# A planned two-branch attention kernel: V products of 512 columns, a limit on filler work, moves of Q and K on two queues, v swapped in one transfer

## The chip, the core and the metric

The kernel runs on one core of a Trainium2 chip. The metric is the device time of one launch in microseconds (us). The kernel before took 2022.6 us (median of three runs, 2015.66 to 2030.31). The engines are named as the profile names them: PE (TensorE, matmuls), PEld (its weight loads), DVE (VectorE), ACT (ScalarE), POOL (GpSimd), SP (SyncE, which here only issues transfers).

## The reference, cut to what matters

Two attention branches over the same x of 2048 rows and 512 columns are mixed row by row by a gate. Both have 32 heads of width 16. In branch a all heads share one k and one v; in branch b each head has its own.

```python
g = sigmoid((x * gate_w).sum(-1, keepdims=True))
# a: q = x @ wq (32 heads), k = x @ wk, v = x @ wv (one head of width 16)
# b: q, k, v = x @ wqkv (32 heads each)
scores = einsum("bhqd,b[h]kd->bhqk", q, k) * 16 ** -0.5
o = einsum("bhqk,b[h]kd->bhqd", softmax(scores), v)
out = g * (o_a @ wo_a) + (1 - g) * (o_b @ wo_b)
```

## The kernel before, in words

The 64 heads of the two branches are eight groups of eight heads, `groups` = a0, b0, a1, b1, ... Each group is worked in four phases (a half of the query rows, times two pairs of heads), so there are 32 phases. A phase has 32 quads: a quad is one tile of 128 keys (16 of them, `c`), in one of two arrangements of rows (`w`). A quad has two scores. One score is eight matmuls of 64x32 weights over 512 columns (L564) into one of two PSUM tiles `sc`, and one exponential of 128x1024 elements on ACT (L571) that writes a `prob` tile. Then the quad's V product (`values`, L612) multiplies v (with columns of ones, which give the denominators) by the quad's two `prob` tiles and adds into a PSUM tile `pair` for the whole phase. The product is in f32; the profile shows each of its matmuls as two instructions with a weight load each. Before the change a quad's V product is made in two pieces of 256 columns (`value_job`, L628).

Some scores don't go to ACT: the planner hands a whole quad to DVE, which makes the exponential from seven vector instructions (L751 to L763). Its matmuls go to the second `pair` tile, the spare bank; its V product is made in four pieces of 128 columns.

All other matmul work also goes through the spare bank, one piece of work at a time. It is kept as *units*: a projection of q, k or v (24 jobs of eight matmuls, L188; `project`, L371), the turning of v by transposes (16 jobs, L420; `turned`, L414), a product with wo (6 jobs, L188; `o_unit`, L445). A projection ends with two DVE instructions (L394, L397) that split the result into two f16 halves `hi` and `lo`, a single pair of buffers. `put` (L380) then lays them into the row order that the scores need by 32 transfers of 32 KB, issued at L352, all by POOL. `hi` and `lo` are free for the next projection when these are done (`free["hilo"]`). For v, `turned` writes `vB[0]` and copies it with its 64-row halves exchanged into `vB[1]` (`swapped`, L191, by SP): two calls, one for each of the two columns blocks that hold v, two transfers each.

After a phase, DVE copies the sum out (L665), SP moves numerators and denominators by ten transfers into tiles `oT` and `dT` (`normalised`, L505), DVE divides. Four `o_unit`s for each half of a group multiply by wo; DVE applies the gate (L471) into one of two `sum` tiles, and POOL adds them to the output in memory by a transfer that accumulates (L481).

Weights come in by SP (L216, L219), POOL splits them into halves (L204 to L206), and SP exchanges their 64-row halves (`halve`, L224, L193). DVE takes their largest value for a range check (L197). A second `_general` kernel stands behind that check and isn't entered here.

The order in which every engine gets its instructions is written by a planner that runs while the kernel is built. It keeps a model of the clocks of PE, DVE, POOL and ACT (`_Plan`, L77) with fixed costs (L44 to L49 and the numbers in the calls), and at each step emits what would fit. `pe_step` (L843) emits a score as soon as the modelled ACT has emptied its PSUM tile. Until then it emits filler work that ends before `limit` (L858), the modelled start of the last exponential plus `SLACK`: V products of ACT's quads first (`mine`), then jobs of units or scores for DVE (`spare`), then V products of DVE's quads (`other`). `spare_job` (L804) prefers a score for DVE to a unit, except when a unit that can start is within `SPARE` of being late by the model (`hurry`, L795). `pick` (L686) chooses the quad for DVE, at times in the next phase. Each engine works its list in order, whatever the real times are.

Of the kernel before, what the change touches and what calls it, by code (L numbers as in the profile page):

```python
# [44 lines left out]
SCORES, HALF, PRODUCT = 215, 430, 215  # L45
SLACK = 400
TO_VEC, FROM_VEC, CHAINED = 255, 150, 130
ISSUE, LANDS = 520, 3200
PROBS, VECS = 6, 7  # L49
# [27 lines left out]
class _Plan:  # L77


    def __init__(self):  # L80
        self.pe = self.dve = self.pool = self.act = 0.0
        self.starts, self.ends, self.ops, self.last = [], [], [], None
# [42 lines left out]
    def on_pool(self, fns, ready, ns):  # L125

        for fn in fns:
            fn()
            self.pool = max(self.pool, ready) + ns
        return self.pool  # L130

    def exp(self, filled):
# [13 lines left out]
def _fast(ctx, tc, x, wq_a, wk_a, wv_a, wo_a, wqkv_b, wo_b, gate_w, out, flag):  # L146
# [63 lines left out]
    def load_w(src, gi, part, queue=nc.sync):  # L210
# [13 lines left out]
        def halve():  # L224
            split_weight(pair[0][:, 0], pair[0][:, 1], w)
            swapped(pair[1], pair[0], nc.sync)

# [9 lines left out]
        def later(t):  # L237
            at = plan.on_pool([halve], t, 3300)
            ready["w" + part, src, gi] = at + LANDS
            plan.vec(lambda: absmax(f"w{part}_{src}", gi, pair[0][:, 0]), 590, 4, at + 500, due=at + 20000)  # L240
# [130 lines left out]
    def project(part, src, gi, half, kind, can, due):  # L371
# [8 lines left out]
        def put(hilo, t):  # L380
            queue = (nc.gpsimd,)
            to = q_tiles(src, gi, half) if part == "q" else k_tiles(gi, half)
            parts = (0, 1, 0, 1) if part == "q" else (0, 0, 1, 1)
            for p in range(4):
                done = plan.on_pool(lay(hilo, to[p], p, parts, queue), t, ISSUE)
                ready[part, src, gi, half, p] = done + LANDS
            free["hilo"] = done + LANDS - 4000
# [26 lines left out]
    def turned(gi, half, hilo, now):  # L414
# [8 lines left out]
        def finish(t):  # L423
# [5 lines left out]
            def then(end):  # L429
                ts = slice(8 * half, 8 * half + 8)  # L430
                swapped(vB[1][:, ts, :, 0], vB[0][:, ts, :, 0], nc.sync)
                swapped(vB[1][:, ts, :, 2], vB[0][:, ts, :, 2], nc.sync)
                free["spare"] = end + FROM_VEC
                free["hilo"] = end
                ready["v", gi, half] = end + LANDS + 1000

            for k in range(4):
                plan.vec(lambda k=k: put(k // 2, k % 2), 330, 1, t + TO_VEC, (), then if k == 3 else None)

        jobs = [(lambda t=t, part=part: job(t, part), 155) for t in range(8) for part in range(2)]  # L440
        units.append(_Unit(jobs, finish, lambda now: True, lambda: 0, f"turn{gi}{half}"))
# [3 lines left out]
    def o_unit(n, half, t, qs, first, last):  # L445
# [14 lines left out]
        def finish(end):  # L460
            def take(e):
# [6 lines left out]
                if e == 0:  # L468
                    state["sum"] = sums[turn[0]]
                    turn[0] ^= 1  # L470
                nc.vector.tensor_scalar(state["sum"][:, e], pair[1][:, e], g, None, op0=ALU.mult)  # L471

            def then(t):
# [4 lines left out]
                if n == 0:  # L478
                    nc.sync.dma_start(dst, state["sum"])
                else:  # L480
                    plan.on_pool([lambda: nc.gpsimd.dma_start(dst, state["sum"], accum_op=ALU.add)], t, 1500)  # L481

            t_ = t
            for e in range(2):
                plan.vec(lambda e=e: take(e), 620, 1, end + TO_VEC, (), then if e else None)

# [4 lines left out]
                     and made(("wo", src, gi), math.inf) <= now and made("gates", math.inf) <= now  # L491
                     and (n + 1 < len(groups) or made("late", math.inf) <= now), lambda: starts_in(due), f"o{n}{half}{t}")

    turn = [0]

    def normalised(n, half, q, raw, now):
# [7 lines left out]
        for m, (part, at, n_rows, to, e) in enumerate(moves):  # L504
            queues[m % len(queues)].dma_start(part[ROWS * e + to :][:n_rows], raw[at : at + n_rows, e])  # L505
        o16 = ops.tile([P, 2, BLK], F16, tag="o16", name=f"o16{n}{half}{q}", bufs=3)
        o16s[n, half, q] = o16
# [119 lines left out]

    def value_job(now, mine):  # L628

# [9 lines left out]
        m, n = going[mine] if mine in going else (min(can), 0)  # L639
        wide = BLK // (2 if mine else 4)  # L640
        ns = HALF * wide * 2 // BLK

        def job():
            values(m, slice(n * wide, (n + 1) * wide))
            going[mine] = m, n + 1
            if (n + 1) * wide == BLK:
                del going[mine]
                summed(m, plan.pe + ns)
# [37 lines left out]
    def pick(now):  # L686
# [9 lines left out]
        elif ph < LASTS:  # L696
            found = [m for m in range(32 * ph + 32, 32 * ph + 64) if m not in vector]
            ph += 1
            if max(laid(ph, NT - 1, phases[ph][2] + e) for e in range(2)) > now:
                return None  # L700
# [142 lines left out]
    def pe_step():  # L843
# [185 lines left out]
    def preload():  # L1029
# [243 lines left out]
```

## Time and profile before

| what | value |
|---|---|
| three runs, median | 2022.6 us |
| the profiled execution's own time | 2003.99 us |
| its span, first to last instruction | 2001.7 us |
| mean granted TensorE clock | 0.980 |
| PE, PEld busy | 1840.3, 1155.0 us |
| ACT, DVE, POOL busy | 1816.2, 1198.4, 542.4 us |
| bytes moved by transfers | 109.73 MB in 140435 packets |

The tables of the profile are read so. The page's fifth part groups instructions by line, engine, operation and tiles: count, busy time, mean duration of one, then the idle time of the engine just before them and what ended it. A row of the waits says who waited for whom: us in total, times, the longest. A row of the timeline is start, duration, engine, line, operation, tiles, shapes, count, and in brackets the idle time before it with what ended it. A row of the windows has, for each engine, busy us and in brackets how many instructions, then the granted clock, the transfers' share and GB/s. A wait ended by "issue" is one for which the profile shows no other engine. PE's matmuls are pipelined: a row's duration overlaps the next one's, so the distance between starts is what a piece of work costs.

### The profile page before, as it was taken

Reading aid. Unit: us, or ns where it says so; the run is one execution under the profiler, and the core shown is the slowest. Engines: PE = TensorE matmul, PEld = TensorE weight load, DVE = VectorE, ACT = ScalarE, POOL = GpSimd, SP = SyncE. Lnnn points to the kernel's source line nnn. Section 1 sums busy time; section 2 is a strip of 40 time slices with the busy share of each in tenths; the row PEclk is TensorE's granted clock in tenths of the full one; section 3 lists DMA queues with packets and bytes.
Section 4 is the critical chain, followed back from the end, with each engine's and each line's share of the span. In section 5 each row is a group of like instructions: output and inputs, shape, how many; then the busy total and the mean of one; then the engine's idle time right before and its main releaser. Section 6 shows DMA issues by size and latency. Waiting matters only on the chain.

```text
span 2001.7 us, 130978 instructions
## 1 busy us (share of the span) xinstructions
PE 1840.3 (92%) x61680; PEld 1155.0 (58%) x61680; DVE 1198.4 (60%) x1352; ACT 1816.2 (91%) x1961; POOL 542.4 (27%) x891
## 2 busy tenths in 40 slices
PE   8999998998999998998999999899799999898995
PEld 5566564555565665655666566555466565555552
DVE  5166521968385734578457752687657775158983
ACT  4899996998999998998999999899799999998994
POOL 4314303451042503325013430353203233034000
PEclk9999999999999999999999999999999999999997
DMA  5222212223132232133224241141402314116011
GB/s 140 47 34 47 68 36 72 46 56 62 30 62 44 50 56 51 37 62 66 47 40 79 43 70 20 40 87 42 76 5 49 64 38 76 32 27 162 15 57 56
DMA packets 140435, 109.73 MB, mean 55 GB/s; under 512 B 86432, under 2 KB 94880, under 8 KB 139888
## 3 DMA queue, kind: packets, MB, share of 16 engines
q0 software_dynamic: 37376, 50.35, 14.6%
q1 hardware_dynamic: 100560, 48.27, 10.2%
q8 instruction: 485, 7.95, 1.6%
q10 hardware_dynamic: 1952, 2.66, 0.4%
q14 instruction: 62, 0.51, 0.1%
HBM read 14.75 MB, written 33.55 MB: 24 GB/s over the span
## 4 chain that ended last, share of the span: by engine, by line
PE 47%; ACT 31%; issue 9%; DVE 6%; POOL 4%; DMA 2%; SPq 1%; ACTq 0%; DVEq 0%; POOLq 0%
ACT prob L571 31%; PE pair L612 23%; PE sc L564 13%; PE pair L188 8%; DVE vec L763 2%; POOL Qa L352 2%; DVE sum L471 1%; DVE vec L751 1%; SPq L505 1%; PE pair L564 1%; POOL K L352 1%; PE pt L265 1%; DMA wqb<-in_B_wqkv_dram 1%; DVE raw L665 0%; DMA oT<-raw 0%
## 5 line engine op out<-in xcount | busy, mean ns | idle before, releaser
L571 ACT ACTIVATE prob<-sc 128x1024 f32<-128x1024 f32 x1946 | 1805.6, 1093 | 128.3 <-PE sc L564 124.4
L612 PE MATMUL pair<-prob,vA 64*32 64x256 f32 x15680 | 695.8, 378 | 16.9 <-issue 15.7
L612 PE MATMUL pair<-prob,vB 64*32 64x256 f32 x15456 | 657.7, 381 | 11.6 <-issue 10.6
L564 PE MATMUL sc<-Qa,kA 64*32 64x512 f16 x7840 | 477.9, 383 | 18.3 <-issue 6.3
L564 PE MATMUL sc<-Qb,K 64*32 64x512 f16 x7728 | 442.6, 388 | 25.7 <-issue 4.2
L612 PEld LDWEIGHTS pair<-prob,vA 64*32 64x32 f32 x15680 | 350.3, 105 | 81.2 <-issue 38.8
L763 DVE SCALAR_TENSOR_TENSOR vec<-vec,vec 128x1024 f32<-128x1024 f32 x306 | 373.3, 1236 | 2.4
L564 PEld LDWEIGHTS <-K 64*32 64x32 f16 x8192 | 209.0, 91 | 282.5 <-issue 210.9
L612 PEld LDWEIGHTS pair<-prob,vB 64*32 64x32 f32 x15456 | 329.5, 106 | 71.4 <-issue 29.2
L564 PEld LDWEIGHTS <-kA 64*32 64x32 f16 x8192 | 213.3, 90 | 212.2 <-issue 157.1
L352 POOL DMA_DIRECT2D K<-hikb x128 | 65.7, 518 | 385.3 <-DVE hikb L394 382.7
L751 DVE TENSOR_SCALAR vec<-pair 128x1024 int32<-128x1024 f32 x102 | 124.1, 1217 | 71.9 <-PE pair L564 71.2
L352 POOL DMA_DIRECT2D Qa<-hiqa x115 | 59.6, 518 | 360.6 <-DVE hiqa L394 348.8
L763 DVE SCALAR_TENSOR_TENSOR vec<-vec 128x1024 f32<-128x1024 f32 x102 | 125.1, 1226 | 1.0
L481 POOL DMA_DIRECT2D out_dram<-sum x48 | 59.7, 1243 | 239.2 <-DVE sum L471 215.3
L511 DVE RECIPROCAL dT<-dT 128x256 f32<-128x256 f32 (+1 forms) x66 | 111.0, 1690 | 18.8 <-DMA dT<-raw 18.8
L352 POOL DMA_DIRECT2D Qb<-hiqb x128 | 66.2, 517 | 200.1 <-DVE hiqb L394 197.8
L471 DVE TENSOR_SCALAR sum<-pair,gate_up 128x512 f32<-128x512 f32 x112 | 78.5, 740 | 50.9 <-PE pair L188 50.7
L665 DVE COPY raw<-pair 128x1024 f32<-128x1024 f32 x32 | 39.1, 1222 | 116.7 <-PE pair L612 116.5
L188 PE MATMUL pair<-w16ob,o 64*32 64x512 f16 x1536 | 92.1, 396 | 15.3 <-ACT o L517 7.0
L188 PE MATMUL pair<-xT,w16kb 64*32 64x512 f16 x1536 | 101.6, 376 | 4.7 <-issue 4.6
L188 PEld LDWEIGHTS <-o 64*32 64x32 f16 x3072 | 60.7, 94 | 64.4 <-issue 27.4
(137 smaller groups left out, 1564.1 us busy)
## 6 DMA issues: line engine op xcount, KB each, us to landing
out_dram<-sum POOLq DMA_DIRECT2D x48, 512.0 KB, 5.9
dT<-raw SPq DMA_DIRECT2D x126, 64.0 KB, 2.7
vB<-vB SPq DMA_DIRECT2D x32, 128.0 KB, 5.1
Qb<-hiqb POOLq DMA_DIRECT2D x128, 32.0 KB, 2.3
Qb<-loqb POOLq DMA_DIRECT2D x128, 32.0 KB, 2.2
K<-hikb POOLq DMA_DIRECT2D x128, 32.0 KB, 2.3
K<-lokb POOLq DMA_DIRECT2D x128, 32.0 KB, 2.3
out_dram<-sum SPq DMA_DIRECT2D x8, 512.0 KB, 4.3
```

The costliest lines, as they stand in the source:

```text
L188: nc.tensor.matmul(outs[n : n + COLS, i], lhs[i][rows(i), n : n + COLS], rhs[i][rows(i)], start=start, stop=stop)
L265: nc.tensor.matmul(pt[rows(i), 2 * c + w, :], x_tiles[k][:, i, at : at + ROWS], ident, start=c % 2 == w == 0, stop=c % 2 == w == 1)
L352: fns.append(lambda q=queues[(8 * p + n) % len(queues)], dst=dst, src=hilo[part][at]: q.dma_start(dst, src))
L471: nc.vector.tensor_scalar(state["sum"][:, e], pair[1][:, e], g, None, op0=ALU.mult)
L481: plan.on_pool([lambda: nc.gpsimd.dma_start(dst, state["sum"], accum_op=ALU.add)], t, 1500)
L511: nc.vector.reciprocal(d[:, c : c + cut], d[:, c : c + cut])
L564: nc.tensor.matmul(bank[a : a + COLS, hh], k[rows(hh), key : key + COLS], Q[src, gi, half, p][rows(hh), j * BLK : (j + 1) * BLK], start=Tr ...
L571: nc.scalar.activation(probs[u], sc, AF.Exp, scale=SCALE / (UP * UP))
L612: nc.tensor.matmul(pair[0][32 * k : 32 * k + 32, i, cols], v[rows(i)], probs[2 * m + k // 2][rows(i), hh, cols], start=first, stop=last)
L665: nc.vector.tensor_copy(state["raw"], full)
L751: nc.vector.tensor_scalar(tile("p").bitcast(I32), pair[1], SCALE / (UP * UP) / math.log(2) * 2.0 ** 23, None, op0=ALU.mult)
L763: nc.vector.scalar_tensor_tensor(p, m if i == 3 else p, VEC[i], m if i else w, op0=ALU.add, op1=ALU.mult)
```

## The change

It has nine parts, most of them in the planner; the arithmetic is the same.

1. `value_job` makes a V product in one piece of 512 columns where the time left until `limit` is 860 ns or more, else in two of 256; this holds for DVE's quads too. `SLACK` goes from 400 to 404.
2. `LATE`: filler work that isn't a V product of ACT's quads must, ahead of a quad's second score (`part[0]` is 1), end before that score can start.
3. Q and K are laid by SP and POOL in turn, 16 transfers each. The model gets a clock of SP.
4. `vB` is exchanged by one call over all columns, two transfers instead of four.
5. The exchange of weights goes from SP to POOL.
6. Modelled costs: 480 and 600 ns for a transfer of POOL and SP (520), 4800 ns for a weight (3300), 60 ns for a job of `turned` (155), 660 ns for the gate (620), 1300 ns for an accumulating transfer (1500).
7. The units of wo wait in the model for one of the two `sum` tiles.
8. `SPARE` goes from 20000 to 10000; a quad of the next phase is given to DVE only if its Q and K have been laid for 3000 ns in the model.
9. The products of the last group wait 30000 instead of 15000 ns in the model for the output that is read back.

```diff
-SLACK = 400
+SLACK = 404
-ISSUE, LANDS = 520, 3200
+ISSUE, ISSUE_SP, LANDS, SUM_LANDS = 480, 600, 3200, 6500
...
+    def on_sp(self, fns, ready, ns):
+
+        for fn in fns:
+            fn()
+            self.sp = max(self.sp, ready) + ns
+        return self.sp
...
         def halve():
             split_weight(pair[0][:, 0], pair[0][:, 1], w)
-            swapped(pair[1], pair[0], nc.sync)
+            swapped(pair[1], pair[0], nc.gpsimd)
...
-            at = plan.on_pool([halve], t, 3300)
+            at = plan.on_pool([halve], t, 4800)
...
         def put(hilo, t):
-            queue = (nc.gpsimd,)
...
-                done = plan.on_pool(lay(hilo, to[p], p, parts, queue), t, ISSUE)
+                fns = lay(hilo, to[p], p, parts, (nc.sync, nc.gpsimd))
+                done = max(plan.on_sp(fns[0::2], t, ISSUE_SP), plan.on_pool(fns[1::2], t, ISSUE))
                 ready[part, src, gi, half, p] = done + LANDS
             free["hilo"] = done + LANDS - 4000
...
-                swapped(vB[1][:, ts, :, 0], vB[0][:, ts, :, 0], nc.sync)
-                swapped(vB[1][:, ts, :, 2], vB[0][:, ts, :, 2], nc.sync)
+                done = plan.on_sp([lambda: swapped(vB[1][:, ts], vB[0][:, ts], nc.sync)], end, 2 * ISSUE_SP)
...
-                ready["v", gi, half] = end + LANDS + 1000
+                ready["v", gi, half] = done + LANDS + 1000
...
-        jobs = [(lambda t=t, part=part: job(t, part), 155) for t in range(8) for part in range(2)]
+        jobs = [(lambda t=t, part=part: job(t, part), 60) for t in range(8) for part in range(2)]
...
+            begin = end + TO_VEC
+            if n + 1 < len(groups):
+                state["turn"] = turn[0]
+                turn[0] ^= 1
+                begin = max(begin, sum_free[state["turn"]])
             for e in range(2):
-                plan.vec(lambda e=e: take(e), 620, 1, end + TO_VEC, (), then if e else None)
+                plan.vec(lambda e=e: take(e), 660, 1, begin, (), then if e else None)
...
+        plan.sp = max(plan.sp, now) + len(moves) * ISSUE_SP
...
-        wide = BLK // (2 if mine else 4)
+        wide = BLK if n == 0 and room >= 2 * HALF else BLK // 2
         ns = HALF * wide * 2 // BLK
...
-            if max(laid(ph, NT - 1, phases[ph][2] + e) for e in range(2)) > now:
+            if max(laid(ph, NT - 1, phases[ph][2] + e) for e in range(2)) + 3000 > now:
                 return None
...
-    JOB, AFTER, SPARE, WORK, EXTRA = 900, 3000, 20000, 1500, 7000
+    JOB, AFTER, SPARE, WORK, EXTRA, LATE = 900, 3000, 10000, 1500, 7000, 0
...
-        mine, other = (lambda: value_job(now, True)), (lambda: value_job(now, False))
+        mine, other = (lambda: value_job(now, True, limit - now)), (lambda: value_job(now, False, limit - now))
...
-            if job and now + job[1] <= limit:
+            if job and now + job[1] <= (limit if get is mine or not part[0] else min(limit, t + LATE)):
                 run(job)
                 return
...
-        ready["late"] = plan.pe + 15000
+        ready["late"] = plan.pe + 30000
```

More of the change, by code (lines that the diff above doesn't have):

```diff
@@ L80, in __init__ @@
     def __init__(self):
-        self.pe = self.dve = self.pool = self.act = 0.0
+        self.pe = self.dve = self.pool = self.sp = self.act = 0.0
         self.starts, self.ends, self.ops, self.last = [], [], [], None
@@ L468, in take @@
                 if e == 0:
-                    state["sum"] = sums[turn[0]]
-                    turn[0] ^= 1
+                    state["sum"] = sums[state["turn"]]
                 nc.vector.tensor_scalar(state["sum"][:, e], pair[1][:, e], g, None, op0=ALU.mult)
@@ L478, in then @@
                 if n == 0:
-                    nc.sync.dma_start(dst, state["sum"])
+                    done = plan.on_sp([lambda: nc.sync.dma_start(dst, state["sum"])], t, ISSUE_SP)
                 else:
-                    plan.on_pool([lambda: nc.gpsimd.dma_start(dst, state["sum"], accum_op=ALU.add)], t, 1500)
+                    done = plan.on_pool([lambda: nc.gpsimd.dma_start(dst, state["sum"], accum_op=ALU.add)], t, 1300)
+                sum_free[state["turn"]] = done + SUM_LANDS
             t_ = t
+            begin = end + TO_VEC
[3 more added lines that the diff above has]
+                begin = max(begin, sum_free[state["turn"]])
             for e in range(2):
-                plan.vec(lambda e=e: take(e), 620, 1, end + TO_VEC, (), then if e else None)
+                plan.vec(lambda e=e: take(e), 660, 1, begin, (), then if e else None)
         made = ready.get
@@ L491, in o_unit @@
                      and made(("wo", src, gi), math.inf) <= now and made("gates", math.inf) <= now
-                     and (n + 1 < len(groups) or made("late", math.inf) <= now), lambda: starts_in(due), f"o{n}{half}{t}")
-    turn = [0]
+                     and (sum_free[turn[0]] <= now + 4000 if n + 1 < len(groups) else made("late", math.inf) <= now), lambda: starts_in(due), f"o{n}{half}{t}")
+    turn, sum_free = [0], [0.0, 0.0]
     def normalised(n, half, q, raw, now):
@@ L626, in summed, with value_job @@
             emptied(t)
-    def value_job(now, mine):
+    def value_job(now, mine, room):
         if mine not in going:
@@ L639, in value_job @@
         m, n = going[mine] if mine in going else (min(can), 0)
-        wide = BLK // (2 if mine else 4)
+        wide = BLK if n == 0 and room >= 2 * HALF else BLK // 2
         ns = HALF * wide * 2 // BLK
         def job():
-            values(m, slice(n * wide, (n + 1) * wide))
-            going[mine] = m, n + 1
-            if (n + 1) * wide == BLK:
+            values(m, slice(n, n + wide))
+            going[mine] = m, n + wide
+            if n + wide == BLK:
                 del going[mine]
```

## The prediction

> **What bounds the kernel now.** I read the page first (busy time, the queues, the costliest groups), then the waits of ACT and of PE, then the windows and the timeline at the longest waits.
>
> ```profile
> span 2001.7 us, 130978 instructions
> PE 1840.3 (92%) x61680; PEld 1155.0 (58%) x61680; DVE 1198.4 (60%) x1352; ACT 1816.2 (91%) x1961; POOL 542.4 (27%) x891
> ...
> q8 instruction: 485, 7.95, 1.6%
> ...
> L571 ACT ACTIVATE prob<-sc 128x1024 f32<-128x1024 f32 x1946 | 1805.6, 1093 | 128.3 <-PE sc L564 124.4
> L612 PE MATMUL pair<-prob,vA 64*32 64x256 f32 x15680 | 695.8, 378 | 16.9 <-issue 15.7
> L612 PE MATMUL pair<-prob,vB 64*32 64x256 f32 x15456 | 657.7, 381 | 11.6 <-issue 10.6
> ```
>
> ACT's exponentials are the bound: 1946 of them. Where nothing disturbs them, they follow each other at 0.915 us: the row below has 29 in 26.69 us, and (26.69 - 1.09) / 28 = 0.914, with the mean of 1.09 us for the one at the edge.
>
> ```profile
> 1356.07 26.69 ACT L571 ACTIVATE prob<-sc 128x1024 f32<-128x1024 f32 x29
> ```
>
> So 1946 x 0.915 = 1781 us is the floor with this number of exponentials. They account for 1805.6 + 128.3 = 1934 us of the span, and 153 us can be had at most; the rest, about 68 us, is the start and the tail, which the change hardly touches. Of the idle time 124.4 us waits for a score. What did PE wait for then?
>
> ```profile
> PE pair L612 <- issue: 31.9, 44, 2.9
> PE pair L564 <- DVE sum L471: 15.8, 3, 8.2
> PE pair L564 <- DMA K<-lokb: 12.6, 8, 3.2
> PE sc L564 <- issue: 10.5, 17, 2.0
> ...
> PE pair L188 <- DVE sum L471: 6.8, 5, 2.0
> ...
> PE pair L188 <- issue: 5.2, 6, 2.6
> ```
>
> Three causes: 47.6 us in 67 waits for no engine ("issue"), 15.8 us behind DVE, 12.6 us for a K that isn't laid yet. A fourth doesn't show here, since PE was busy with other work: one wait of ACT of 14.86 us (below). Each is met by a part of the change.
>
> **The V product in one piece.** An undisturbed slot, score to score:
>
> ```profile
> 1402.25 0.41 PE L564 MATMUL sc<-Qb,K 64*32 64x512 f16 x8
> 1402.46 0.63 PE L612 MATMUL pair<-prob,vB 64*32 64x256 f32 x16
> 1402.89 0.41 PE L188 MATMUL pair<-w16ob,o 64*32 64x512 f16 x8
> 1403.16 0.41 PE L564 MATMUL sc<-Qb,K 64*32 64x512 f16 x8
> ```
>
> Score 0.21, half a V product 0.43, a filler job 0.22 and 0.05 of waiting: 0.91 us with 8 + 16 + 8 = 32 matmuls and as many loads. No row has a V matmul of 512 columns; I take it at twice that of 256, so a whole product is 0.86 us in 16 matmuls, and PE's working time doesn't change. Bounds: 0.82 (the loads cost something now) to 0.90. What changes is the count: 2 slots hold 16 + 16 + 16 = 48 matmuls instead of 64. The q8 row moves 7.95 MB in 485 packets, 16.4 KB each, and PE's 61680 + 61680 instructions over 485 are 254 to a packet: I read it as PE's instruction stream. A packet lasts 254 / 64 x 0.91 = 3.6 us now and 254 / 96 x 1.83 = 4.8 us after, so each next packet may be 1.2 us later before PE runs dry. The longest of the waits named issue:
>
> ```profile
> 482.76 0.37 PE L564 MATMUL sc<-Qb,K 64*32 64x512 f16 x1 [2.00 <-issue]
> ...
> 1172.23 0.44 PE L612 MATMUL pair<-prob,vA 64*32 64x256 f32 x4 [2.87 <-issue]
> ...
> 1833.86 0.43 PE L612 MATMUL pair<-prob,vB 64*32 64x256 f32 x6 [1.70 <-issue]
> ...
> 1452.50:1455.70 3.20, 3.20 (x78) 2.93 (x75) 3.20 (x4) 1.48 (x2) 0.00 (x0) 0.50 0.02 5
> ```
>
> Ten of these are longer than 1.2 us (first, longest and last shown), 21 us together; shortened by 1.2 each they leave 9, and the shorter ones vanish. That is 47.6 - 9 = 39 us gained, between 0 (the waits aren't this) and 48. After a long wait the granted clock stands at 0.50 for some 3.2 us (last row), in which PE, which has 6% to spare, falls behind by up to 1.6 us; fewer long waits of this and the next causes save about five such windows, 8 us.
>
> The Trainium skill, "Runtime: NRT & Kernel Launch", section Instruction fetch mechanics, says that instructions come in blocks of 16 KiB which the sequencer fetches while it runs the block before, and that crossing a block is mostly hidden. The size agrees with the 16.4 KB of the q8 row; by "mostly hidden" the 47.6 us would be something else, which is a rival below.
>
> The price: a quad's first score now comes behind 0.86 us of V product, not 0.43. By the model's own constants a score at the limit (404) is followed by its exponential at 404 + 456 = 860 of 904 ns, so a delay of over 44 ns ahead of it reaches ACT whole, at some 970 quads; before, 0.05 us of waiting stood ahead of every score. Bounds: 0, and 970 x 0.04 = 39 us if the piece is 0.90. I take 8, near the first, because the slot's parts repeat to 0.01 us.
>
> **Q and K on two queues.** 32 transfers of one put take POOL 15 to 16 us, and the next projection waits for them: in both stretches below PE has no projection at all (third and fourth row), and that is what is missing when ACT then waits for K at 306 us.
>
> ```profile
> 88.50:106.50 18.00, 16.47 (x32) 1.00 0.32 62
> 173.50:190.40 16.90, 15.25 (x31) 1.00 0.37 81
> ...
> 88.50:106.50 18.00, 0.00 (x0) 0.14 (x8) 1.00 0.32 62
> 173.50:190.40 16.90, 0.00 (x0) 0.13 (x8) 1.00 0.37 81
> ...
> 310.08 1.23 DVE L394 TENSOR_SCALAR hikb<-pair 128x1024 f16<-128x1024 f32 x1 [17.41 <-PE pair L188]
> ...
> 321.54 1.02 ACT L571 ACTIVATE prob<-sc 128x1024 f32<-128x1024 f32 x1 [14.86 <-PE sc L564]
> ...
> L352 SPq DMA_DIRECT2D Qa<-hiqa x11: 507/587/1549, 22.0 to 32.0; - x11
> ```
>
> On two queues SP needs 16 x 0.59 = 9.4 us (last row) and POOL 16 x 0.48 = 7.7, so hi and lo are free 6 us earlier. Two such steps ahead of 306 us and K itself 3 to 5 us earlier for its second pair cover most of the 14.86 us: I take 10, between 0 and 15. The K that DVE's quads wait for (12.6 us, the next phase's) comes 4 to 6 us earlier as well and is picked only 3 us after it is laid: 11 of 12.6.
>
> What stands in the way is SP's own list: behind 9.4 us of laying, a phase's sums move late.
>
> ```profile
> 477.50 2.46 SPq L505 DMA_DIRECT2D dT<-raw  x4
> 480.00 4.18 SPq L505 DMA_DIRECT2D oT<-raw  x6
> ...
> DVE dT L511 <- DMA dT<-raw: 18.8, 6, 5.0
> ```
>
> DVE waits for `dT` in order (last row), and behind it stand the instructions that free the spare bank. 23 puts of 9.4 us cover 216 of some 1900 us, so 3 or 4 of 31 phases meet one, with about 3 us each beyond what is planned: +6 in the sum, up to 25.
>
> **Weights exchanged by POOL.** The wait of 8.2 us, in order:
>
> ```profile
> 1406.61 1.11 SPq L193 DMA_DIRECT2D w16vb<-w16vb  x2
> 1407.81 0.53 SPq L219 DMA_DIRECT2D wqb<-in_B_wqkv_dram  x1
> 1410.91 1.49 POOL L204 TENSOR_SCALAR wqb<-wqb 128x512 f32<-128x512 f32 x1 [4.33 <-DMA wqb<-in_B_wqkv_dram]
> 1413.12 0.69 DVE L197 TENSOR_REDUCE stats<-w16qb 128x1 f32<-128x512 f16 x1 [7.07 <-POOL w16qb L205]
> 1413.72 1.40 DVE L471 TENSOR_SCALAR sum<-pair,gate_up 128x512 f32<-128x512 f32 x2
> 1415.17 0.72 PE L564 MATMUL pair<-Qb,K 64*32 64x512 f16 x8 [8.20 <-DVE sum L471]
> ```
>
> SP can't issue the next load before the exchange ahead of it, which waits for POOL's split; so POOL waits for the load, DVE in its list for POOL, the spare bank for DVE, and PE stops. Without the exchange on SP the load goes out while POOL splits the weight before, some 6 us earlier. I take 15 of the 15.8 us. POOL pays two transfers a weight, 1.1 us, and is 27% busy; what covers it is that idle time, and a Q or K put behind it would be 1.1 us late.
>
> **v in one exchange** saves two issues of SP a time, 16 x 2 x 1.1 us in all on a queue that mostly waits: nothing in the sum. It should take the 64-byte packets away.
>
> ```profile
> DMA packets 140435, 109.73 MB, mean 55 GB/s; under 512 B 86432, under 2 KB 94880, under 8 KB 139888
> ```
>
> **The planner's other numbers** change how often DVE takes a score. Each score more is 0.915 us less of ACT. Shorter turning jobs in the model, hi and lo free earlier and units held back to 10 us before they are due all leave the spare bank free more often; the 3000 ns and `LATE` take some away. I take 8 scores more than the 102 there are now (seven vector instructions each, DVE 60% busy): -7 us, between +15 and -25. The later units of wo (`sum` tiles, the output read back) delay no score: what covers them is the last half group's exponentials, and without that cover the tail grows by a unit's six jobs and its gate, 6 x 0.22 + 1.40 = 2.7 us. Nothing in the sum.
>
> **The sum.** -39 - 8 + 8 (V in one piece) - 10 - 11 + 6 (two queues) - 15 (weights) - 7 (planner) = -76 us. The profiled execution took 2003.99 us, so 1928 for one like it. The median of the runs is 2022.6, 18.6 above it; with the same distance, 1947 us.
>
> **The rivals.**
> *More for DVE.* If the planner finds 45 more scores for DVE, not 8, and ACT's waits shrink by 10 more, it is 1947 - 37 x 0.915 - 10 = 1903 us. For it: DVE is 60% busy. Against: DVE's quads need a spare bank that the units hold most of the time. 0.17.
> *The stream isn't the cause.* The issue waits have another reason, or whole pieces are rarely made because the 860 ns must fit exactly: then the 39 and the 8 are lost and it is 1947 + 47 = 1994. This is what the page's "mostly hidden" comes to. For it: PE stops within a group where no row shows a reason. Against: 254 instructions to a packet. 0.13.
> *Slower: units begun too late.* With `SPARE` halved, scores for DVE go ahead of projections for 10 us longer; if K or Q then comes late at each of the eight groups, PE stops as at 306 us. Price: 8 x 14.86 = 119 us against the gain of 76: 1947 + 119 = 2066. It decides from a stop of 76 / 8 = 9.5 us a group. For it: the plan ran late once already with 20000. Against: each put is 6 us shorter, and that single wait is the only one of its size. 0.12.
> *No difference.* The waits move: V pieces make the first scores late by their whole bound (39 - 8 = 31), and SP's list costs its 25 (19 more than taken), and whole pieces save half: 1947 + 31 + 19 + 23 = 2020. 0.08.
>
> **How the numbers follow.** My forecast, most of the waits going, has 0.50; its own range is 1915 to 1980, from the bounds of its terms. The range from 1888 to 2008 takes in the rival with more for DVE and the one without the stream and leaves out the slower one, most of the case without difference, and the edge of the first: under 2 in 10. One per cent, what a measurement of this kernel can tell from no change, is 20 us: faster than 2002 holds the forecast, the first and nearly all of the second rival: 0.79; within it 0.09; slower 0.12.
>
> **What the profile after would show.** The q8 packets fall from 485 to 360 to 390, the V groups show 64x512 with half the matmuls, and waits named issue fall under 15 us; if the packets fall and the waits stay, the stream isn't the cause. The row K from `lokb` and the 8.2 us behind `sum` vanish; if not, the two queues or the order on SP are misread. Packets under 512 B fall by about 65000. ACT has 1930 to 1945 exponentials; waits of PE for K, Q or xT at the start of groups would speak for the slower rival, and DVE waiting longer for `dT` for SP's list being full.

## The result and the profile after

The changed kernel takes 1888.0 us (median of four runs, 1883.59 to 1889.3) against 2026.5 us for the kernel before in the same session (2015.66 to 2032.98): a ratio of 0.932, with a 95% interval of 0.927 to 0.937. The gain is 138 us where 76 were forecast. The profiled execution took 1883.59 us, and the two profiled spans, 2001.7 and 1881.8 us, differ by 119.9. One run of the experiments, the fourth of `e7_v_strided`, took 2900 us at a granted clock of 0.556 and is left out.

From the page of the changed kernel, the rows that answer to those of before:

```profile
span 1881.8 us, 97974 instructions
PE 1761.2 (94%) x45072; PEld 849.9 (45%) x45072; DVE 1217.6 (65%) x1380; ACT 1797.6 (96%) x1957; POOL 380.8 (20%) x569
...
DMA packets 74067, 109.71 MB, mean 58 GB/s; under 512 B 20640, under 2 KB 29088, under 8 KB 73648
...
q8 instruction: 355, 5.82, 1.3%
...
L583 ACT ACTIVATE prob<-sc 128x1024 f32<-128x1024 f32 x1942 | 1787.0, 1077 | 23.9 <-PE sc L576 22.4
L624 PE MATMUL pair<-prob,vA 64*32 64x512 f32 (+1 forms) x8112 | 524.8, 577 | 0.1
L624 PE MATMUL pair<-prob,vB 64*32 64x512 f32 (+1 forms) x7984 | 517.4, 574 | 1.6 <-issue 1.4
```

Lines have moved (L571 is L583, L564 is L576, L612 is L624, L188 is L195, L471 is L476). ACT still has the same work, 1942 exponentials for 1946, and its wait for scores fell from 124.4 to 22.4 us. Exponentials with the idle time before them take 1787.0 + 23.9 = 1810.9 us where they took 1933.9: 123 us less, while the rest of the span went from 67.8 to 70.9. So the whole gain lies in the stretch of the exponentials, as forecast. 104 of the 123 us are idle time; the other 19 are busy time, in part because an exponential adds 1.02 us after a break and 0.92 right behind another, and 121 waits for a score became 22. ACT's floor, 1942 x 0.915, is 1777 us, and 34 us are left above it. PE, with fewer and wider instructions, is busier in share and freer in fact: its waits now begin with ACT.

The waits of PE, longest in total first:

```profile
PE sc L576 <- ACT prob L583: 58.2, 166, 0.9
PE pair L576 <- DMA K<-lokb: 8.8, 6, 1.6
...
PE pair L576 <- DVE sum L476: 1.7, 1, 1.7
PE pair L624 <- issue: 1.4, 1, 1.4
...
PE sc L576 <- issue: 0.9, 3, 0.5
...
PE pair L195 <- issue: 0.2, 1, 0.2
```

The three rows named issue fell from 47.6 to 2.5 us, the scores' wait behind `sum` (L471 before) from 15.8 to 1.7, K from `lokb` only from 12.6 to 8.8. New on top are 58.2 us in which PE waits until ACT has emptied a score tile: it is ahead of ACT now.

A whole V product in the timeline, with a score on each side, and a stretch of ACT:

```profile
1253.64 0.41 PE L576 MATMUL sc<-Qb,K 64*32 64x512 f16 x8
1253.85 1.05 PE L624 MATMUL pair<-prob,vB 64*32 64x512 f32 x16
1254.71 0.41 PE L576 MATMUL sc<-Qb,K 64*32 64x512 f16 x8
...
1256.49 44.37 ACT L583 ACTIVATE prob<-sc 128x1024 f32<-128x1024 f32 x48 [0.16 <-ACT prob L583]
```

16 matmuls of 512 columns last 1254.71 - 1253.85 = 0.86 us, as taken. The price of 8 us for first scores that come late isn't to be seen: in the last row 48 exponentials follow each other at (44.37 - 1.08) / 47 = 0.92 us, through whole products and fillers alike.

### The profile page after: what moved, and what is told of

It is laid out like the page before. It is cut to its first block, busy times and chain, and to the rows that moved or that the text cites. A ratio compares the mean times of both kernels' runs of the same rounds, so it can differ in the third digit from the quotient of the medians.

```text
span 1881.8 us, 97974 instructions
## 1 busy us (share of the span) xinstructions
PE 1761.2 (94%) x45072; PEld 849.9 (45%) x45072; DVE 1217.6 (65%) x1380; ACT 1797.6 (96%) x1957; POOL 380.8 (20%) x569
## 4 chain that ended last, share of the span: by engine, by line
ACT 67%; PE 16%; issue 12%; DVE 3%; DMA 1%; SPq 1%; POOL 0%; ACTq 0%; DVEq 0%; POOLq 0%
ACT prob L583 67%; PE pair L624 7%; PE sc L576 4%; PE pair L195 3%; DVE vec L775 1%; PE pt L272 1%; DMA K<-lokb 0%; SPq L516 0%; SPq L359 0%; DVE xT L470 0%; DVE sum L476 0%; PE pair L272 0%; DMA oT<-raw 0%; DMA vec<-in_A_x_dram 0%; PE pair L300 0%
## 5 line engine op out<-in xcount | busy, mean ns | idle before, releaser
L583 ACT ACTIVATE prob<-sc 128x1024 f32<-128x1024 f32 x1942 | 1787.0, 1077 | 23.9 <-PE sc L576 22.4
L624 PE MATMUL pair<-prob,vA 64*32 64x512 f32 (+1 forms) x8112 | 524.8, 577 | 0.1
L624 PE MATMUL pair<-prob,vB 64*32 64x512 f32 (+1 forms) x7984 | 517.4, 574 | 1.6 <-issue 1.4
L576 PE MATMUL sc<-Qb,K 64*32 64x512 f16 x7696 | 408.4, 382 | 44.7 <-ACT prob L583 36.2
L576 PE MATMUL sc<-Qa,kA 64*32 64x512 f16 x7840 | 407.7, 380 | 29.1 <-ACT prob L583 22.1
L576 PEld LDWEIGHTS <-K 64*32 64x32 f16 x8192 | 203.3, 90 | 434.0 <-issue 396.0
L576 PEld LDWEIGHTS <-kA 64*32 64x32 f16 x8192 | 202.7, 89 | 408.4 <-issue 366.9
L624 PEld LDWEIGHTS pair<-prob,vB 64*32 64x32 f32 x7984 | 156.5, 105 | 23.7 <-issue 4.2
L624 PEld LDWEIGHTS pair<-prob,vA 64*32 64x32 f32 x8112 | 155.2, 105 | 20.0 <-issue 2.0
L476 DVE TENSOR_SCALAR sum<-pair,gate_up 128x512 f32<-128x512 f32 x112 | 78.3, 738 | 75.1 <-PE pair L195 75.1
L523 DVE RECIPROCAL dT<-dT 128x256 f32<-128x256 f32 (+1 forms) x66 | 111.5, 1693 | 20.3 <-DMA dT<-raw 20.3
L359 POOL DMA_DIRECT2D Qa<-loqa x122 | 59.5, 495 | 294.2 <-DVE loqa L404 238.7
L359 POOL DMA_DIRECT2D Qb<-loqb x128 | 65.4, 519 | 236.2 <-PE sc L576 235.5
L359 POOL DMA_DIRECT2D K<-hikb x64 | 33.3, 520 | 253.8 <-DVE hikb L401 253.8
L195 PE MATMUL pair<-w16ob,o 64*32 64x512 f16 x1536 | 64.4, 391 | 14.5 <-ACT o L529 6.8
```

The lines of the kernel that those rows point to most:

```text
L195: nc.tensor.matmul(outs[n : n + COLS, i], lhs[i][rows(i), n : n + COLS], rhs[i][rows(i)], start=start, stop=stop)
L359: fns.append(lambda q=queues[(8 * p + n) % len(queues)], dst=dst, src=hilo[part][at]: q.dma_start(dst, src))
L523: nc.vector.reciprocal(d[:, c : c + cut], d[:, c : c + cut])
L576: nc.tensor.matmul(bank[a : a + COLS, hh], k[rows(hh), key : key + COLS], Q[src, gi, half, p][rows(hh), j * BLK : (j + 1) * BLK], start=Tr ...
L583: nc.scalar.activation(probs[u], sc, AF.Exp, scale=SCALE / (UP * UP))
L624: nc.tensor.matmul(pair[0][32 * k : 32 * k + 32, i, cols], v[rows(i)], probs[2 * m + k // 2][rows(i), hh, cols], start=first, stop=last)
```

## The experiments

Each kernel is the changed one with one edit, except `e5_before_whole`, which is the kernel before with two of the nine parts. The kernel before ran beside them: 2017.0 us (e1 to e4), 2009.1 (e5, e6, e8, e9), 2021.4 (e7, e10, e11, e12). "Wait" is ACT's wait for scores in the profiled execution, "stops" the idle time named issue ahead of the weight loads of V products (PEld), DVE's scores are those that go to DVE in place of ACT.

| kernel | us | ratio to before (95%) | q8 packets | wait | stops | DVE's scores |
|---|---|---|---|---|---|---|
| before | | 1 | 485 | 124.4 | 78.3 | 102 |
| changed | 1888.0 | 0.932 (0.927 to 0.937) | 355 | 22.4 | 6.1 | 106 |
| e1_halves | 1965.2 | 0.973 (0.969 to 0.977) | 472 | 82.3 | 55.9 | 106 |
| e2_quarters | 2822.9 | 1.397 (1.389 to 1.405) | 728 | 854.8 | 701.0 | 106 |
| e5_before_whole | 1899.7 | 0.945 (0.942 to 0.948) | 355 | 38.9 | 3.3 | 100 |
| e9_no_late | 1913.4 | 0.951 (0.947 to 0.955) | 413 | 58.9 | 30.8 | 122 |
| e12_slack400 | 2013.4 | 0.996 (0.994 to 0.999) | 461 | 152.0 | 64.3 | 104 |
| e3_lay_pool | 1886.1 | 0.934 (0.930 to 0.938) | 355 | 20.6 | 4.9 | 102 |
| e4_weights_sp | 1886.4 | 0.934 (0.930 to 0.938) | 355 | 26.9 | 5.4 | 106 |
| e10_both | 1893.6 | 0.936 (0.933 to 0.940) | 355 | 29.6 | 6.1 | 102 |
| e8_pick_laid | 1890.6 | 0.940 (0.937 to 0.943) | 354 | 18.6 | 6.6 | 98 |
| e6_spare20 | 1887.9 | 0.941 (0.937 to 0.945) | 355 | 17.6 | 6.0 | 96 |
| e11_filtered_916 | 1894.7 | 0.936 (0.934 to 0.938) | 354 | 34.2 | 8.4 | 110 |
| e7_v_strided | 1882.7 | 0.930 (0.926 to 0.934) | 355 | 18.1 | 2.5 | 106 |

**Is it the instruction stream?** `e1_halves` keeps the plan, so the order of all work, and only issues each whole V product as two of 256 columns.

```diff
-            values(m, slice(n, n + wide))
+            for a in range(n, n + wide, BLK // 2):
+                values(m, slice(a, a + BLK // 2))
```

> The changed kernel with the same plan, but each V product that is planned in one piece of 512 columns is issued as two of 256 directly behind each other: the same work in the same order, with as many V instructions as the kernel before. Theory (the stream of PE's instructions was the largest cost, and fewer instructions took it away): packets of q8 back to 470 to 485, waits of PE named issue back to 25 to 60 us, time 1945 to 1970 us, which is 60 to 80 above the changed kernel. Rival (the order of the work made the gain, not the number of instructions): 1888 us within 10, waits named issue under 10 us.

It took 77 us more than the changed kernel (spans: 1955.6 against 1881.8). From its page and its waits of PE:

```profile
q8 instruction: 472, 7.73, 1.7%
```

```profile
PE sc L576 <- ACT prob L583: 53.6, 153, 1.0
PE pair L624 <- issue: 25.3, 29, 2.3
PE sc L576 <- issue: 9.2, 9, 2.0
```

The product itself isn't slower in 32 matmuls than in 16: from the start of the V row to the next score it is 0.86 us in both kernels. In e1:

```profile
1292.01 1.06 PE L624 MATMUL pair<-prob,vB 64*32 64x256 f32 x32
1292.87 0.42 PE L576 MATMUL sc<-Qb,K 64*32 64x512 f16 x8
```

Nothing else differs, so the number of instructions costs the 74 to 77 us. The rival that the stream isn't the cause falls here.

`e2_quarters` issues them as four of 128 (`BLK // 4`): twice as many V matmuls as in e1, with the same columns in all.

> The same with pieces of 128 columns, a doubling of the suspected cost: two slots hold 96 matmuls and 96 loads, 192 of 254 instructions to a packet, so a packet lasts 2.4 us. In the kernel before 13 packets came in a stretch of 50 us without a wait, one in 3.8 us. Theory: packets can't come every 2.4 us, PE is bound by its instructions all the way, and the time is over 2300 us with some 700 packets. Rival (order): 1888 to 1920 us.

2822.9 us, 1.397 times the kernel before. Its page, its waits of PE, and one stop in its timeline:

```profile
span 2818.2 us, 193462 instructions
...
q8 instruction: 728, 11.93, 1.8%
```

```profile
PE pair L624 <- issue: 568.6, 467, 4.1
PE sc L576 <- issue: 115.2, 120, 2.9
```

```profile
1000.96 0.86 PE L624 MATMUL pair<-prob,vA 64*32 64x128 f32 x36
1004.18 0.55 PE L624 MATMUL pair<-prob,vA 64*32 64x128 f32 x22 [2.37 <-issue]
```

PE stops 2.37 us inside one V product of 64 matmuls, between its 36th and its 37th, which works on the same tiles: no data is missing, so it is the instructions. Here the stream sets the time: 2818.2 / 728 = 3.87 us a packet; single distances go from 3.2 us up, and half are under 3.74. The changed kernel asks for a packet in 1881.8 / 355 = 5.30 us; e1, with its 472 packets, would need one in 3.99 to be as fast. The kernels in order of the distance, which holds the stops themselves: e2 3.87, before 2001.7 / 485 = 4.13, e1 4.14, e12 4.40, e9 4.63, changed 5.30, e5 5.35. The stops in the table fall in the same order, but for e12, and are nearly gone at 5.3. The Trainium skill, "Runtime: NRT & Kernel Launch", section Instruction fetch mechanics, calls the crossing of a block of 256 instructions mostly hidden; on these runs that holds at 5.3 us a block and fails at 4.1.

**How much do parts 1 and 2 do alone?** `e5_before_whole` is the kernel before with `SLACK` 404, the new `value_job` and the limit `LATE`, and nothing else.

```diff
-SLACK = 400
+SLACK = 404
...
-    def value_job(now, mine):
+    def value_job(now, mine, room):
...
-        wide = BLK // (2 if mine else 4)
+        wide = BLK if n == 0 and room >= 2 * HALF else BLK // 2
...
-            if job and now + job[1] <= limit:
+            if job and now + job[1] <= (limit if get is mine or not part[0] else min(limit, t + LATE)):
```

> The kernel before with the first two parts of the change alone: pieces of 512 where 860 ns are left, the limit ahead of a second score, 404. Theory: this takes the waits for instructions, about 75 us, and nothing else; the waits behind DVE's sum, for K from lokb and at the first K stay as before, so 1940 to 1955 us with 350 to 380 packets of q8. Rival (the other parts bring nothing by themselves; exchanging weights by SP and laying by POOL in the changed kernel left its time the same): 1885 to 1905 us.

1899.7 us, within the rival's range and 40 us below the theory's: the two parts bring 103 of the 120 us of span (2001.7 to 1898.6), and 0.055 of the ratio's 0.068. Where is the rest? This is the stretch near 300 us that the prediction spoke of, from the timelines of e5, of the changed kernel and of `e3_lay_pool` (below):

```profile
307.19 1.02 ACT L571 ACTIVATE prob<-sc 128x1024 f32<-128x1024 f32 x1 [8.34 <-PE sc L564]
311.84 23.94 ACT L571 ACTIVATE prob<-sc 128x1024 f32<-128x1024 f32 x26 [3.62 <-PE sc L564]
```

```profile
302.28 1.02 ACT L583 ACTIVATE prob<-sc 128x1024 f32<-128x1024 f32 x1 [1.46 <-PE sc L576]
304.14 31.68 ACT L583 ACTIVATE prob<-sc 128x1024 f32<-128x1024 f32 x34 [0.83 <-PE sc L576]
```

```profile
305.80 1.02 ACT L583 ACTIVATE prob<-sc 128x1024 f32<-128x1024 f32 x1 [3.61 <-PE sc L576]
310.36 4.93 ACT L583 ACTIVATE prob<-sc 128x1024 f32<-128x1024 f32 x5 [3.53 <-PE sc L576]
316.29 19.36 ACT L583 ACTIVATE prob<-sc 128x1024 f32<-128x1024 f32 x21 [1.01 <-PE sc L576]
```

ACT waits 12.0 us there in e5, 2.3 in the changed kernel, 8.2 in e3. That is 9.7 of the 16.8 us between e5 and the changed kernel; the six more scores for DVE (106 for 100) are 6 x 0.915 = 5.5.

**Without the limit `LATE`** (`LATE` infinite) fillers may again stand ahead of a second score, and V products are cut more often.

```diff
-    JOB, AFTER, SPARE, WORK, EXTRA, LATE = 900, 3000, 10000, 1500, 7000, 0
+    JOB, AFTER, SPARE, WORK, EXTRA, LATE = 900, 3000, 10000, 1500, 7000, math.inf
```

> The changed kernel without the limit ahead of a second score (filler work may end at the common limit). Theory: fillers then push the second score to the limit, 860 ns don't fit behind it, V products come in halves again: packets of q8 420 to 480, time 1920 to 1965 us. Rival (whole pieces are made anyway): packets within 10 of 355, 1888 within 10.

1913.4 us with 413 packets, both a little below what was expected, and the stops are back with the packets.

```profile
PE pair L624 <- issue: 11.3, 14, 1.7
```

DVE takes 122 scores, so ACT has 16 exponentials fewer (15 us), and it is still 25 us slower than the changed kernel (31 by span): the stops, and some new waits for DVE, cost 40 to 46.

**With `SLACK` back at 400** whole products must fit into 4 ns less.

```diff
-SLACK = 404
+SLACK = 400
```

> The changed kernel with SLACK at 400 instead of 404: in the model 857 ns are left behind a second score, where a whole product takes 860. Theory: nearly every V product comes in halves, packets of q8 450 to 480, waits named issue 30 us and more, 1940 to 1975 us. Rival: enough whole pieces fit elsewhere, under 1910 us.

2013.4 us: all but 8 of the 138 us are gone, and the time lies 38 us above the range of the theory (its packets lie within). The profiled execution was the slowest of its ten runs (2029.4). From its groups with shapes kept apart, its page, and its waits of PE:

```profile
L624 PE MATMUL pair<-prob,vA 64*32 64x256 f32 x14656 | 618.4, 379 | 14.2 <-issue 14.2
```

```profile
q8 instruction: 461, 7.55, 1.6%
```

```profile
PE pair L624 <- issue: 20.7, 23, 2.5
PE pair L195 <- DVE vec L763: 20.1, 4, 7.3
PE pair L576 <- DVE vec L763: 12.4, 3, 6.0
```

Most V products are in two pieces again, and the packets with them. It is worse than e1, which has more packets, and the plan differs too: 32.5 us of PE's waits are for DVE's exponentials (last two rows), which the changed kernel hasn't. So this run shows what 4 ns in the model decide, not the cost of the instructions alone.

**The two queues and the weights.** `e3_lay_pool` lets POOL alone lay Q and K, the plan knowing it.

```diff
-                fns = lay(hilo, to[p], p, parts, (nc.sync, nc.gpsimd))
-                done = max(plan.on_sp(fns[0::2], t, ISSUE_SP), plan.on_pool(fns[1::2], t, ISSUE))
+                fns = lay(hilo, to[p], p, parts, (nc.gpsimd,))
+                done = plan.on_pool(fns, t, ISSUE)
```

> The changed kernel with Q and K laid by POOL alone again, the plan told so (480 ns each). Theory of the prediction: the wait at the first K comes back (10 to 15 us), the waits for K from lokb grow by 4 to 8 us, together 1905 to 1915 us. Rival (two queues bring nothing, since transfers share their way and the projections wait for other things): 1888 within 8.

1886.1 us: no difference, as the rival had it. Inside, three things go against each other: at 300 us ACT waits 8.2 us, not 2.3 (rows above); DVE takes 4 scores fewer (3.7 us); but PE's 8.8 us of waits for K from `lokb` fall to 0.7 in this plan. The Trainium skill, "DMA: Bandwidth & Descriptors", section Issuing engines are not separate DMA queues, says that issuing from several engines saves only the time of issuing. The trace agrees: the K of 722 us is laid in 10.0 us from first to last issue on two queues (722.3 to 732.3) and in 17.2 on one (722.5 to 739.7), and the kernel's time doesn't depend on it.

`e4_weights_sp` gives the exchange of weights back to SP.

```diff
-            swapped(pair[1], pair[0], nc.gpsimd)
+            swapped(pair[1], pair[0], nc.sync)
```

> The changed kernel with the exchange of weights on SP again, same plan. Theory: SP holds each next load back until POOL has split the weight before, DVE waits for POOL and PE for the spare bank: waits of PE behind DVE's sum up by 10 to 20 us, 1898 to 1910 us. Rival (the wait went because POOL lays only half of Q and K now and comes to the weights earlier): 1888 within 6, waits behind sum under 5 us.

1886.4 us, no difference; PE's waits behind `sum` rise from 1.7 to 4.8 us, not to 15:

```profile
PE pair L576 <- DVE sum L476: 4.8, 2, 3.6
```

`e10_both` makes both edits, since one might cover the other.

> The changed kernel with the exchange of weights on SP and Q and K laid by POOL alone, both at once. Theory (each of the two alone keeps the weights early enough, so undoing one did nothing): now POOL comes late to the weights and the loads wait for the exchange, the waits behind DVE's sum return, 10 to 18 us of ACT, 1896 to 1908 us. Rival (neither matters; the wait went through the planner's 4800 ns for a weight): 1886 within 6.

1893.6 us lies between the two expected ranges: 5.6 us above the changed kernel, with a ratio of 0.936 whose interval overlaps that of the changed kernel, so a cost isn't shown. Waits behind `sum` don't come back (1.7 us), ACT's waits at 300 us are 7.6.

**The planner's choice.** In the changed kernel a wait of ACT after K is laid:

```profile
722.30 0.51 SPq L359 DMA_DIRECT2D K<-hikb  x1
...
725.84 0.40 PE L576 MATMUL pair<-Qb,K 64*32 64x512 f16 x4 [1.53 <-DMA K<-lokb]
...
727.57 0.61 PE L576 MATMUL pair<-Qb,K 64*32 64x512 f16 x4 [1.33 <-DMA K<-lokb]
...
728.72 1.02 ACT L583 ACTIVATE prob<-sc 128x1024 f32<-128x1024 f32 x1 [3.28 <-PE sc L576]
```

A score for DVE (its output is `pair`) stands in PE's list while K is still being laid, and ACT waits 3.28 us behind it. `pick` asks whether K is laid only for quads of the next phase. `e8_pick_laid` asks it for both.

```diff
             found = [m for m in range(at[0] + 2, 32 * ph + 32) if m not in vector]
+            if max(laid(ph, NT - 1, phases[ph][2] + e) for e in range(2)) + 3000 > now:
+                return None
```

> The changed kernel, and a score for DVE out of the same phase is picked only when its K has been laid for 3000 ns in the model (as for the next phase). Theory: the waits for K from lokb that are left (8.8 us in 6 waits, three stretches at half clock) come from picks in the same phase, whose last quads need the second half of K while it is being laid; they vanish, 1874 to 1881 us. Rival: DVE loses as many scores as the waits cost, 1888 within 4.

All waits for K are gone, and the time is 1890.6 us, not better: DVE's groups in the changed kernel and in e8 show why.

```profile
L763 DVE TENSOR_SCALAR vec<-pair 128x1024 int32<-128x1024 f32 x106 | 128.7, 1214 | 75.2 <-PE pair L576 74.9
```

```profile
L765 DVE TENSOR_SCALAR vec<-pair 128x1024 int32<-128x1024 f32 x98 | 119.1, 1215 | 62.2 <-PE pair L576 62.0
```

Eight scores fewer for DVE are eight exponentials more for ACT, 7.3 us, while ACT's waits for scores fall by only 3.8 (22.4 to 18.6): the 8.8 us that PE waited for K had cost ACT less than half of that.

`e6_spare20` puts `SPARE` back to 20000.

> The changed kernel with SPARE at 20000 again. Theory: the number of scores on DVE (106) and the waits hardly depend on it, 1888 within 8. Rival (SPARE is what removed the wait at the first K or brought the scores on DVE): over 1900 us, scores on DVE under 98 or a wait of over 5 us at a group's start.

1887.9 us, the same time, but with 96 scores for DVE, not about 106 as the theory had it: ten exponentials more (9.2 us), of which ACT's shorter waits (17.6 us for 22.4) make up half; the profiled spans are 3.7 us apart. So `SPARE` does bring scores to DVE, as the rival had it, but hardly any time. The prediction's slower rival's condition isn't there with 10000 either: ACT's longest wait for a score in the changed kernel is 3.3 us, where it needed 9.5 a group.

`e11_filtered_916` was meant to beat both kernels: the model's exponential at 916 ns, as measured, and `pick` taking the last quad whose K is laid.

```diff
-EXP, EXP_ENDS, EXP_AFTER = 904, 1136, 456
+EXP, EXP_ENDS, EXP_AFTER = 916, 1136, 456
...
-            found = [m for m in range(at[0] + 2, 32 * ph + 32) if m not in vector]
+            found = [m for m in range(at[0] + 2, 32 * ph + 32) if m not in vector and max(laid(ph, quads[m][1], phases[ph][2] + e) for e in range(2)) + 3000 <= now]
...
-        if len(found) < 33 - MOST:
+        if not found or sum(1 for m in range(32 * ph, 32 * ph + 32) if m in vector) >= MOST:
```

> A version meant to beat the changed kernel: a score for DVE out of the same phase is the last quad whose K has been laid for 3000 ns in the model (not the last quad of the phase), and the model's exponential takes 916 ns, the distance measured, not 904. Theory: the waits for K from lokb go without losing scores on DVE (110 instead of 106), 9 + 4 us less, 1870 to 1878 us. Rival: the plan with 916 ns is slower than ACT in places and gives it back, 1888 within 5.

1894.7 us, above both expected ranges: DVE takes 110 scores, no wait of PE for K is left, and in their place PE waits for DVE. ACT's two longest waits, 9.6 and 5.4 us, follow such stops of 3.2 and 1.6 us and the projection that stands behind them.

```profile
PE pair L195 <- DVE vec L763: 5.3, 4, 3.2
...
PE pair L624 <- DVE vec L775: 2.9, 1, 2.9
```

**v in four strided transfers**, as before the change:

```diff
-                done = plan.on_sp([lambda: swapped(vB[1][:, ts], vB[0][:, ts], nc.sync)], end, 2 * ISSUE_SP)
+                done = plan.on_sp([lambda: [swapped(vB[1][:, ts, :, d], vB[0][:, ts, :, d], nc.sync) for d in (0, 2)]], end, 2 * ISSUE_SP)
```

> The changed kernel with v exchanged by four strided transfers instead of two, same plan. Theory: packets under 512 B rise from 20640 to about 86000 and the time stays, 1888 within 6. Rival (the small packets hold up the packets of instructions): waits of PE named issue over 15 us, over 1900 us.

1882.7 us (median of three): 65792 more small packets are back, 65536 of them of 64 bytes, and cost nothing that can be measured. No version here is clearly faster than the changed kernel.

## Why the prediction was right in direction and short by 62 us

The forecast was 1947 us for the median, from a profiled execution of 1928; measured are 1888.0 and 1883.6. So 44 of the 59 us between the medians lie in the sum, and 14 in the step that put the median 18.6 us above the profiled execution, as it was before: it is 4.4 above it now. The rest of the 62 us is the kernel before, 2026.5 here and 2022.6 when the forecast was made. (Kernels with stops spread more from run to run: before 2015.66 to 2032.98, `e12_slack400` 2008.26 to 2029.42, changed 1883.59 to 1889.3; whether the stops do that wasn't tested.) The forecast's own range, 1915 to 1980, was missed. That the wider range, from 1888, just holds the result is luck: it reached so low for the rival with more for DVE, which didn't come.

**V in one piece: the term that was mis-sized.** Forecast: -39 for the waits named issue, -8 for the half clock after them, +8 for late first scores, -39 together. Measured by e1: -74 in span, -77 in time. The cause was right (packets 485 to 355, just below the forecast; 16096 V matmuls of ACT's quads for 31136), its size wasn't, in two places of the working. The half clock has little part in it: by the trace's record of the clock, the stretches at 0.50, without the one at the end, went from 54.6 us in all to 13.7, twelve windows of 3.41 us and not five, but e1 has 23.9, only three windows more than the changed kernel.

First, the prediction treated the stream as late packets, each to be forgiven 1.2 us, though its own working had the sign of a limit: 3.6 us a packet in a slot with a filler, where e2 shows that packets come at 3.87 on average. A row of such slots could not hold its pace. With whole products it can: 5.30 us a packet, and the stops are nearly gone.

Second, 47.6 us were the wrong rows to count. PE's matmul records overlap each other, so a stop shorter than the overlap leaves no idle time. The weight loads don't hide it. From the waits of PEld before and after:

```profile
PEld pair L612 <- issue: 78.3, 124, 3.4
PEld L188 <- issue: 49.5, 89, 3.1
```

```profile
PEld L195 <- issue: 15.7, 34, 2.0
...
PEld pair L624 <- issue: 6.1, 12, 1.9
```

In V products and projections, where loads have no tile to wait for, 78.3 + 49.5 = 127.8 us before fell to 21.8. Not all of that reaches ACT, but before the change the 127.8 us were there to be read. e1 has 55.9 + 18.6 = 74.5 us in these two rows, 52.7 more than the changed kernel, for a loss of 74 us. What ACT lost is seen from the starts of all exponentials: against one every 0.915 us it falls behind by 158 us before, 114 in e1 and 39 after, and 114 - 39 = 75 us is e1's whole loss. The same three matmul rows that gave 47.6 us give 34.7 in e1.

The price of +8 didn't come: PE is ahead of ACT (58.2 us of waits for a tile), so the score behind a whole product finds room. What the rival without the stream named as a condition, whole pieces rarely made because 860 ns must fit exactly, did come with 400 ns of slack (e12).

**The first K, -10.** It came, 15 us: ACT waited 14.9 us and 2.4 for the next there before, 2.3 in all after. It goes with the two queues in part: with them and half pieces (e1) the two waits are 1.65 and 0.69 us, with POOL alone (e3) 8.2 in all, with the two V parts alone (e5) 12.0. In e3 the time doesn't change, so in the end the queues are worth nothing here.

**K for DVE's quads, -11.** Only about 4 came (12.6 to 8.8). The step said that a K is picked only 3 us after it is laid; that holds for quads of the next phase alone, and the rest are of the same phase (722 us above). e8 takes them away and gains nothing.

**SP's list, +6.** Not seen: DVE's wait for `dT` is 20.3 us in 5 waits, for 18.8 in 6.

```profile
DVE dT L523 <- DMA dT<-raw: 20.3, 5, 5.1
```

**Weights, -15.** The waits behind `sum` went from 15.8 to 1.7 us, but not by the exchange: with it back on SP they are 4.8 us (e4), with both moves back 1.7 (e10). In e5, with nothing but parts 1 and 2 and the weights as they were, they are 4.9. The chain at 1406 us was real in that plan; the plans of e4, e5 and e10 don't have it.

**The planner, -7.** Four scores more, 3.7 us, not eight.

The terms don't add up. Of the 120 us of span, parts 1 and 2 bring 103 alone (e5). The whole plan with its V products issued in halves (e1) keeps 46, and a plan that makes halves by itself (e12) keeps 8 us of time. The smaller terms were waits that more than one part removes. The rival with more for DVE was wrong, although it gave 1903: 106 scores, not 147. Which of the seven small parts makes up the 17 us beyond e5 isn't settled part by part; none that was undone singly (e3, e4, e6, e7) costs a measurable amount, and parts 6, 7 and 9 and the 3000 ns of part 8 weren't tried alone.

## What to carry to other kernels

Divide the time by the packets of PE's instruction queue: where that comes near the distance at which packets can come (3.9 us for 254 instructions here; stops were still there at 4.6 and nearly gone at 5.3), the number of PE's instructions is a bound of its own, and wider matmuls pay even when they do the same work in the same time. Read such stops from the weight loads, since matmul records hide the short ones. In a plan with fixed limits ask by how many ns the new piece fits, and try the step that undoes it.

## What the runs showed of the hardware that wasn't expected

- PE's instructions come in packets of 16.4 KB at about 3.87 us each when nothing else limits (e2). After a late packet starts, PE resumes 2.2 to 3.0 us later, at 399 of e2's 412 stops of over 1 us, worked out from the starts of q8's packets and of PE's next matmuls. The packet's own transfer takes 1.1 us of that on average. Packet n (from 0) starts when PE has started some 256 n + 230 matmuls and loads in the changed kernel and 256 n + 340 in e2, all the way through (medians), so it looks as if a packet is asked for each time PE has used one up; that is a reading of two traces, not a test. Why a packet takes that long, and whether other transfers slow it, stays open.
- 65536 more packets of 64 bytes in SBUF cost nothing that can be measured (e7).
- Exponentials of 128x1024 that last 1.02 us alone follow each other at 0.92 (1256 us above), so ACT's floor is not its mean duration times their number. Nor is the distance one number: those under 0.94 us have a mean of 0.908 us before, most near 0.904, and of 0.915 in the changed kernel, most near 0.921. Over 1857 distances that is 13 us of ACT's time; what makes it isn't known.
